# Linear attention and two dense layers on one core: a block's scores behind its outputs and state, five blocks ahead of the layers

## The chip, the cores and the metric

The kernel runs on one core of one Trainium2 chip. The metric is the device time in microseconds of one execution of the whole program. The engines of the core work side by side, each on a queue of its own: TensorE (PE) multiplies matrices, VectorE (DVE), ScalarE (ACT) and GpSimd (POOL) do the elementwise work, and SyncE (SP) starts the transfers. An instruction begins when those ahead of it on its engine have been issued and when the data and buffers that it needs are free; semaphores tell it so.

## The reference, cut to what matters

Attention runs in blocks of 64 positions with a state per head that decays from block to block; its output goes through two dense layers with different activations.

```python
for b in range(nb):                                  # 12 blocks of 64
    qb, kb, vb = (q[:, :, sl], k[:, :, sl], v[:, :, sl])
    intra = np.einsum('bhic,bhjc->bhij', qb, kb) * Dmask[None]
    intra = np.einsum('bhij,bhjd->bhid', intra, vb)
    inter = np.einsum('bhid,bhde->bhie', qb * lam_pow[None], kv_state)
    out[:, :, sl] = intra + inter
    kb_dec = kb * rev_pow[None]
    kv_state = lam_block[None, :, None, None] * kv_state + np.einsum('bhsd,bhse->bhde', kb_dec, vb)
...
x = out as (1536, 512)
h = x @ w_in;   x = np.where(h > 0, h, np.exp(np.minimum(h, 0)) - 1) @ w_out      # layer 1
h = x @ w2_in;  out = (np.maximum(h, 0) + alpha * np.minimum(h, 0)) @ w2_out      # layer 2
```

There are 2 sequences of 768 positions, 8 heads of 64; the layers are 512 to 2048 to 512 wide. The weights are doubles, the rest are floats.

## The kernel before

**Attention.** The recurrence does not depend on the block's length, and the kernel takes blocks of 128 positions: 12 of them, 6 for each sequence. Heads are taken in 4 pairs. For a block n, `scores` (L201, tile `sc`) multiplies keys and queries on PE into two PSUM banks, one for each head of the pairs; `mask` (L208, tile `sm`) multiplies each bank by the decay on DVE and frees it. `outputs` (tile `po`) adds on PE what comes from the state (L249, with the scaled queries `qs_t`) and what comes from the masked scores (L255). `keep` then splits the result in two parts of the type fp32r, which the layers multiply: ACT casts it to the high part `xh` (L267), DVE subtracts that to get the low part `xl` (L268). `state` (L222, tile `stp`) multiplies scaled keys `kd_t` and values on PE; ACT scales the old state (L230) and DVE adds the new part (L236), or copies it at a sequence's first block (L234). `scale` makes `kd_t` (L182) and `qs_t` (L189) on POOL. A block's keys and queries are one load of 0.5 MB, its values and natural keys a second one of 0.5 MB (0.25 MB in a sequence's last block).

**Layers.** Each layer has 4 groups of 4 chunks of the hidden width, 3 tiles of 512 tokens: 48 items a layer, 96 in all, in the order group, tile, chunk. An item's `up` is 12 matmuls of 512 columns (L355): high weights `wih` times high x, and the two mixed products `wil` times `xh` and `wih` times `xl`. ACT takes relu and exp (L366, L369), DVE makes `g_t` (L370), ACT its high part `gh_t` (L376), POOL its low part `gl_t` (L377). An item's `down`, two items later (LAG), is 12 matmuls of the same kind (L393, tile `dn`).

**Weights.** They come in 32 pieces of 1 MB, 8 for each of the four matrices, as pairs of 32-bit words of a double. `split_w` makes two float parts of such a piece with six operations: ACT scales the upper word (L125), DVE shifts and merges in three operations (L126, L128, L131, tile `wt`), ACT casts to the high part `wih` or `woh` (L134), POOL subtracts for the low part `wil` or `wol` (L135). The arguments `first` and `gaps` say how many ticks later each of the six is put in the program. Each piece's first matmuls in the layers wait for it; pieces 0 and 2 are the first two of `w_in`, 1 and 3 the first two of `w_out`.

**The order.** The program is written out in order, without a scheduler. A count of ticks goes up inside `up` (4 ticks), after each part of `down` (4 for an item), and a few times a block ahead of the layers; `later(n, step)` puts a step n ticks on. The first AHEAD blocks run before the first item; then each of the first items is `up(i)`, the block AHEAD + i, and `down(i - 2)`. `weights(i)` starts the splits of the table `when` at item i (negative ones during the blocks ahead), with the times of the table `early`, and the loads of later pieces.

**Buffers.** All eight PSUM banks are in one ring: scores take two, outputs, state and `up` one each, the `down` of four chunks of one tile four. A bank is given out again when the operations that read it are done: the masks for scores, cast and `xl` for outputs, addition or copy for state.

`begin` starts the loads, builds the decays (`dm` and `qp`, by scans on DVE), does scores, scaling and mask of block 0, the scaling of block 1, the state of block 0, and starts the split of piece 0. The functions that the change touches, and what calls them:

Of the kernel before, what the change touches and what calls it, by code (L numbers as in the profile page):

```python
# [15 lines left out]
NBLK = B * S // C  # L16
# [10 lines left out]
NG = 4  # L27
GF = NF // NG
LAG = 2
AHEAD = 4  # L30


@with_exitstack
def attention_two_layers(
# [13 lines left out]
    nc = tc.nc  # L48
# [16 lines left out]
    def bank(name):  # L65
        return ps.tile([128, 512], F32, tag="ps", name=name)
# [14 lines left out]
    def later(n, step):  # L81
        if n:
            due.setdefault(clock[0] + n, []).append(step)
        else:
            step()
# [52 lines left out]
    xh = {}  # L138
# [17 lines left out]
    st = [st2[:, 0], st2[:, 1]]  # L156
# [4 lines left out]
    def load(n):  # L161


        t = accp.tile([128, 4, 512], F32, tag="acc", name="blk")
        z = t[:, 0:2].rearrange("p s (a i) -> p s a i", a=NP)
        nc.sync.dma_start(out=z, in_=kqT[n])
        m = 2 if n % PB != PB - 1 else 1
        u = t[:, 2:4].rearrange("p s (h d) -> p s h d", h=H)
        nc.sync.dma_start(
            out=u[:, 0:m], in_=vk[n, :, 0:m, :].rearrange("j a (h d) -> j a h d", h=H))  # L170
        ld[n] = z
        vs[n] = (u[:, 0], u[:, 1] if m > 1 else None)
# [21 lines left out]
    def scores(n):  # L194
        z = ld[n]

        ps_ = [bank("sc"), bank("sc")]
        for pr in range(NP):
            for hs in range(2):
                a, b = hs * 64, (hs + 1) * 64  # L200
                nc.tensor.matmul(  # L201
                    out=ps_[hs][:, pr * C:(pr + 1) * C], lhsT=z[a:b, 0, pr, :],
                    rhs=z[a:b, 1, pr, :], start=True, stop=True)
        sc[n] = ps_

    def mask(n):
        for hs, p_ in enumerate(sc.pop(n)):
            nc.vector.tensor_tensor(  # L208
                out=sms[n % 2][:, hs], in0=p_.rearrange("p (a i) -> p a i", a=NP),
                in1=dm[:, hs], op=ALU.mult)  # L210
# [60 lines left out]
    def run_up(n):  # L271
        pw = bank("warm")
        for _ in range(n):
            nc.tensor.matmul(out=pw[:, 0:C], lhsT=warm, rhs=warm, start=True, stop=True)  # L274

    def block(n):

        if n + 1 < NBLK:
            scores(n + 1)
            mask(n + 1)  # L280
        keep(n, outputs(n))
        for _ in range(3 if n < AHEAD else 0):
            tick()
        if n + 1 < NBLK:
            state(n + 1)
        if n + 4 < NBLK:
            load(n + 4)
        if n + 2 < NBLK:
            scale(n + 2)

    def begin():
        nc.sync.dma_start(out=row[:, 128:128 + H], in_=lam.rearrange("h a -> a h"))
        load(0)
        load(1)
        load(2)
        load_w(0)
        load(3)
        nc.vector.memset(warm, 0.0)
        nc.vector.memset(row[:, 0:128], 1.0)

        nc.gpsimd.memset(anti, 0.0)
        nc.gpsimd.affine_select(
            out=anti, in_=anti, pattern=[[1, C]], base=1 - C, channel_multiplier=1,
            compare_op=ALU.not_equal, fill=1.0)
        nc.scalar.activation(fill[:, 0:1], warm[:, 0:1], AF.Exp)
        run_up(3)

        p_ = bank("lamp")
        nc.tensor.matmul(
            out=p_[:, 0:H], lhsT=row[:, 0:128], rhs=row[:, 128:128 + H], start=True, stop=True)  # L310
        run_up(5)
        nc.vector.tensor_copy(lam_sb, p_[:, 0:H])
        for hs in range(2):
            a, b = hs * 64, (hs + 1) * 64
            nc.vector.tensor_copy(
                lamp[a:b, 0:NP], lam_sb.rearrange("p (a s) -> p s a", s=2)[a:b, hs])


        for hs in range(2):
            for pr in range(NP):  # L320
                h = 2 * pr + hs
                nc.vector.tensor_tensor_scan(  # L322
                    out=dm[:, hs, pr, :], data0=lam_sb[:, h:h + 1].to_broadcast([128, C]),
                    data1=anti, initial=0.0, op0=ALU.mult, op1=ALU.add)

        for pr in range(NP):
            nc.vector.tensor_tensor_scan(
                out=qp[:, pr, :], data0=lamp[:, pr:pr + 1].to_broadcast([128, C]),
                data1=warm, initial=1.0, op0=ALU.mult, op1=ALU.add)
        for s_ in st:  # L330
            nc.gpsimd.memset(s_, 0.0)
        scores(0)
        scale(0)
        mask(0)
        scale(1)
        state(0)
        split_w(0, (8, 9, 11, 13, 15), 7)


    gh = {}  # L340
# [4 lines left out]
    def up(i):  # L345
        l, q, t, f = items[i]
        wh, wl = split[2 * (l * NPAIR + f // 2)]
        fo = (f % 2) * 128
        p_ = bank("up")
        n = 0  # L350

        rest = [(wl, xh), (wh, xl)]
        for w, x in [(wh, xh)] + (rest if f % GF == 0 else rest[::-1]):
            for cc in range(NCC):
                nc.tensor.matmul(  # L355
                    out=p_, lhsT=w[:, cc, fo:fo + 128], rhs=x[t][:, cc, :],
                    start=n == 0, stop=n == 3 * NCC - 1)
                n += 1
                if n % 3 == 0:
                    tick()  # L360
        g = tmp.tile([128, CH], F32, tag="g", name="g_t", bufs=3)
        r = tmp.tile([128, CH], F32, tag="r", name="r_t", bufs=3)
        gh_ = gp.tile([128, CH], F32R, tag="gh", name="gh_t")
        gl_ = gp.tile([128, CH], F32R, tag="gl", name="gl_t")
        gh[i], gl[i] = gh_, gl_
        nc.scalar.activation(r, p_, AF.Relu, scale=-1.0)  # L366
        if l == 0:

            nc.scalar.activation(r, r, AF.Exp, scale=-1.0)  # L369
            later(1, lambda: nc.vector.scalar_tensor_tensor(  # L370
                out=g, in0=r, scalar=-1.0, in1=p_, op0=ALU.add, op1=ALU.max))
        else:

            later(1, lambda: nc.vector.scalar_tensor_tensor(  # L374
                out=g, in0=r, scalar=beta[:, f:f + 1], in1=p_, op0=ALU.mult, op1=ALU.add))
        later(2, lambda: nc.scalar.copy(gh_, g))  # L376
        later(3, lambda: nc.gpsimd.tensor_tensor(  # L377
            out=gl_, in0=g, in1=gh_.bitcast(F32), op=ALU.subtract))
# [46 lines left out]
    PER = NCH * GF  # L425

    when = {-1: [2], 0: [1], 2: [3]}
    early = {2: ((6, 7, 9, 11, 13), 5), 1: ((2, 4, 6, 8, 10), 1)}
    for g in range(1, 2 * NG):
        o = (g - 1) * PER  # L430

# [4 lines left out]
    def weights(i):  # L436
        for c in when.get(i, []):
            split_w(c, *early.get(c, ()))
            if c + 3 < 4 * NPAIR:
                later(10, lambda c=c: load_w(c + 3))  # L440

    def parts(i, e):

# [3 lines left out]

    with tc.manual_schedule():
        begin()
        for n in range(AHEAD):  # L450
            weights(n - AHEAD)
            block(n)
# [6 lines left out]
        for i, _ in enumerate(items):  # L459
            if i == 2:  # L460
                nc.sync.dma_start(out=alpha_sb, in_=alpha)
            if i == 20:
                nc.vector.tensor_scalar(
                    out=beta, in0=alpha_sb, scalar1=-1.0, scalar2=1.0, op0=ALU.mult,
                    op1=ALU.add)
            n = AHEAD + i
            up(i)
# [63 lines left out]
```

## Time and profile before

| | before |
|---|---|
| median of 3 runs | 588.08 us (588.04 to 588.97) |
| profiled execution | 588.86 us, of which the span of the core's work 586.9 |
| PE | 573.2 us busy, 98% of the span, 2958 matmuls |
| weight loads of PE | 475.8 us, 81% (beside the matmuls) |
| DVE | 275.8 us, 47% |
| ACT | 240.9 us, 41% |
| POOL | 231.3 us, 39% |
| mean granted clock | 0.994 of full |

The busy shares are means over the span. Cut in 40 slices of 14.7 us, PE is at 80 to 90% in the first two, at 60% in the third and at 90% or more in nearly all others; the granted clock is full but for the first slice and the fifth (58.7 to 73.4 us). DVE and POOL are busiest, and the transfers fullest (331 to 415 GB/s), in the first three slices. What PE waits for thus lies in the first 60 us, where the 12 blocks, the loads and the first splits meet.

How to read the views used below: the list of waits has, for each engine and line, what ended its idle time, with the total in us, the number of times and the longest. The chain of work is followed back from the last instruction, and shows what ran one after the other up to there. A timeline lists the instructions of an engine with start and duration, and in brackets the idle time ahead and what ended it. A table of windows has busy times of stretches. "x16" for scores is 8 matmuls in 16 records.

### The profile page before, as it was taken

What the parts mean: (1) busy time and instruction counts of PE and PEld (TensorE: products, weight loads), DVE (VectorE), ACT (ScalarE), POOL (GpSimd) and SP (SyncE); (2) the same over time, 40 slices, a digit from 0 to 9 for tenths busy, and PEclk for the clock granted to TensorE, in tenths of its full rate; (3) what the DMA queues carried; (4) which work ended last, traced back from release to release, by engine and by line L of the source; (5) the groups of instructions that cost most, each with busy time, mean ns of one, the idle gap of its engine ahead of it and who ended that gap; (6) DMA issues with size and microseconds to landing.
All of it is one profiled execution on the core that took longest, in us unless ns stands there. A gap on an engine that the chain in (4) does not pass through costs nothing.

```text
span 586.9 us, 7331 instructions
## 1 busy us (share of the span) xinstructions
PE 573.2 (98%) x2958; PEld 475.8 (81%) x2958; DVE 275.8 (47%) x363; ACT 240.9 (41%) x374; POOL 231.3 (39%) x156
## 2 busy tenths in 40 slices
PE   8896999999999999999999999999999999999997
PEld 7685888888888888888888888888888888888886
DVE  7877343654535443453646632443543541541332
ACT  2645343656444444445554542443324322432220
POOL 4685421445333443443243444344325334432221
PEclk9999899999999999999999999999999999999999
DMA  8994200433102212221012222122203110000111
GB/s 331 415 353 162 69 1 1 143 95 120 43 29 73 71 73 71 73 71 73 16 56 71 73 71 73 71 74 71 73 0 126 30 60 0 2 0 1 71 73 71
DMA packets 18307, 49.23 MB, mean 84 GB/s; under 512 B 1250, under 2 KB 1506, under 8 KB 18274
## 3 DMA queue, kind: packets, MB, share of 16 engines
q1 hardware_dynamic: 18274, 48.77, 23.4%
q8 instruction: 23, 0.38, 0.2%
q14 instruction: 10, 0.08, 0.0%
HBM read 45.62 MB, written 3.15 MB: 83 GB/s over the span
## 4 chain that ended last, share of the span: by engine, by line
PE 92%; POOL 3%; DMA 2%; issue 1%; DVE 1%; ACT 0%; DVEq 0%; POOLq 0%; SPq 0%
PE dn L393 44%; PE up L355 43%; DMA blk<-in_kqT 2%; PE po L255 1%; POOL kd_t L182 1%; PE sc L201 1%; PE po L249 1%; POOL qs_t L189 1%; POOL gl_t L377 1%; PE stp L222 1%; DVE dm L322 0%; DVE acc L409 0%; POOL wol L135 0%; PE warm L274 0%; POOL wil L135 0%
## 5 line engine op out<-in xcount | busy, mean ns | idle before, releaser
L377 POOL TENSOR_TENSOR gl_t<-g_t,gh_t 128x512 fp32r<-128x512 f32 x96 | 125.7, 1309 | 327.3 <-ACT gh_t L376 274.6
L366 ACT ACTIVATE r_t<-up 128x512 f32<-128x512 f32 x96 | 57.3, 597 | 184.9 <-PE up L355 184.9
L376 ACT CAST gh_t<-g_t 128x512 fp32r<-128x512 f32 x96 | 59.6, 621 | 114.0 <-DVE g_t L370 60.9
L409 DVE TENSOR_TENSOR acc<-dn,acc 128x512 f32<-128x512 f32 (+1 forms) x73 | 47.0, 678 | 75.7 <-PE dn L393 75.7
L393 PE MATMUL dn<-gh_t,woh 128*128 128x512 f32 x192 | 76.3, 397 | 0.2 <-DVE xl L268 0.2
L374 DVE SCALAR_TENSOR_TENSOR g_t<-r_t,beta,up 128x512 f32<-128x512 f32 x48 | 35.7, 743 | 86.2 <-ACT r_t L366 77.4
L393 PE MATMUL dn<-gl_t,woh 128*128 128x512 f32 x192 | 75.5, 393 | 0.0
L393 PE MATMUL dn<-woh,gl_t 128*128 128x512 f32 (+1 forms) x196 | 75.5, 385 | 0.0
L393 PE MATMUL dn<-woh,gh_t 128*128 128x512 f32 (+1 forms) x196 | 75.5, 385 | 0.0
L393 PE MATMUL dn<-wol,gh_t 128*128 128x512 f32 (+1 forms) x196 | 75.4, 385 | 0.0
L393 PE MATMUL dn<-gh_t,wol 128*128 128x512 f32 x192 | 75.4, 393 | 0.0
L370 DVE SCALAR_TENSOR_TENSOR g_t<-r_t,up 128x512 f32<-128x512 f32 x48 | 32.9, 685 | 63.2 <-ACT r_t L369 58.7
L355 PE MATMUL up<-xh,wih 128*128 128x512 f32 x192 | 51.7, 391 | 0.0
L355 PE MATMUL up<-yh,wih 128*128 128x512 f32 x192 | 51.4, 389 | 0.0
L355 PE MATMUL up<-xl,wih 128*128 128x512 f32 x192 | 51.4, 389 | 0.0
L355 PE MATMUL up<-xh,wil 128*128 128x512 f32 x192 | 51.4, 389 | 0.0
L355 PE MATMUL up<-yl,wih 128*128 128x512 f32 x192 | 51.3, 389 | 0.0
L355 PE MATMUL up<-yh,wil 128*128 128x512 f32 x192 | 51.3, 389 | 0.0
L126 DVE TENSOR_SCALAR wt<-wt 128x1024 uint32<-128x1024 uint32 x32 | 31.4, 982 | 33.7 <-ACT wt L125 33.6
L393 PEld LDWEIGHTS dn<-gh_t,woh 128*128 128x128 f32 x192 | 36.6, 190 | 8.8 <-issue 0.6
L393 PEld LDWEIGHTS dn<-woh,gh_t 128*128 128x128 f32 x196 | 36.8, 188 | 7.4
L393 PEld LDWEIGHTS dn<-woh,gl_t 128*128 128x128 f32 x196 | 36.8, 188 | 7.4
(57 smaller groups left out, 797.2 us busy)
## 6 DMA issues: line engine op xcount, KB each, us to landing
raw<-in_w1i SPq DMA_DIRECT2D x8, 1024.0 KB, 5.8
raw<-in_w1o SPq DMA_DIRECT2D x8, 1024.0 KB, 4.8
raw<-in_w2i SPq DMA_DIRECT2D x8, 1024.0 KB, 5.3
raw<-in_w2o SPq DMA_DIRECT2D x8, 1024.0 KB, 4.8
blk<-in_kqT SPq DMA_DIRECT2D x12, 512.0 KB, 6.5
blk<-in_vk SPq DMA_DIRECT2D x10, 512.0 KB, 7.7
out<-acc SPq DMA_DIRECT2D x11, 256.0 KB, 2.1
blk<-in_vk SPq DMA_DIRECT2D x2, 256.0 KB, 6.4
```

Source lines behind the costliest of these rows:

```text
L126: later(gaps[0], lambda: nc.vector.tensor_scalar(out=tu, in0=tu, scalar1=3, scalar2=None, op0=ALU.logical_shift_left))
L182: nc.gpsimd.tensor_tensor(out=kd_.rearrange("p (a s) d -> p a s d", s=2), in0=kk.rearrange("p (a s) d -> p a s d", s=2), in1=rev.to_broadc ...
L189: nc.gpsimd.tensor_tensor(out=qs_, in0=q_, in1=qp, op=ALU.mult)
L201: nc.tensor.matmul(out=ps_[hs][:, pr * C:(pr + 1) * C], lhsT=z[a:b, 0, pr, :], rhs=z[a:b, 1, pr, :], start=True, stop=True)
L355: nc.tensor.matmul(out=p_, lhsT=w[:, cc, fo:fo + 128], rhs=x[t][:, cc, :], start=n == 0, stop=n == 3 * NCC - 1)
L366: nc.scalar.activation(r, p_, AF.Relu, scale=-1.0)
L370: later(1, lambda: nc.vector.scalar_tensor_tensor(out=g, in0=r, scalar=-1.0, in1=p_, op0=ALU.add, op1=ALU.max))
L374: later(1, lambda: nc.vector.scalar_tensor_tensor(out=g, in0=r, scalar=beta[:, f:f + 1], in1=p_, op0=ALU.mult, op1=ALU.add))
L376: later(2, lambda: nc.scalar.copy(gh_, g))
L377: later(3, lambda: nc.gpsimd.tensor_tensor(out=gl_, in0=g, in1=gh_.bitcast(F32), op=ALU.subtract))
L393: nc.tensor.matmul(out=p_, lhsT=a, rhs=b, start=first and n == 0, stop=last and n == 2)
L409: nc.vector.tensor_tensor(out=a, in0=p_, in1=a, op=ALU.add)
```

## The change

Four things are moved; no arithmetic is added or taken away.

- **Scores.** `block(n)` did scores and mask of block n+1 ahead of the outputs of block n. Now it does so only for n < AHEAD; from there on they stand behind the state of block n+1, that is last in the block on PE, and the mask stands behind `xl` and the state addition on DVE. Scores and mask of block 1 go into `begin`, ahead of the first state; the scans for `qp` go behind the mask of block 0.
- **AHEAD** is 5 instead of 4, so item i goes with block i + 5.
- **First weights.** The split of piece 0 starts 16 ticks on instead of 7, behind the fourth block; block 3 is loaded ahead of piece 0. The splits of pieces 2 and 1 have new times in `early`, and since piece 2's start is tied to AHEAD it comes one block later too. Later weight loads are issued 11 ticks behind a split's start instead of 10.
- **Order within `up`.** The two mixed products came with `wil` first in each group's first chunk and with `xl` first otherwise; now `wil` comes first only in the first chunk of the second layer.

```diff
-AHEAD = 4
+AHEAD = 5
...
+    def next_scores(n):
+        if 1 < n < NBLK:
+            scores(n)
+            mask(n)
+
     def block(n):
 
-        if n + 1 < NBLK:
-            scores(n + 1)
-            mask(n + 1)
+
+        if n < AHEAD:
+            next_scores(n + 1)
         keep(n, outputs(n))
         for _ in range(3 if n < AHEAD else 0):
             tick()
         if n + 1 < NBLK:
             state(n + 1)
+        if n >= AHEAD:
+            next_scores(n + 1)
         if n + 4 < NBLK:
             load(n + 4)
...
         load(2)
+        load(3)
         load_w(0)
-        load(3)
...
-        for pr in range(NP):
-            nc.vector.tensor_tensor_scan(
-                out=qp[:, pr, :], data0=lamp[:, pr:pr + 1].to_broadcast([128, C]),
-                data1=warm, initial=1.0, op0=ALU.mult, op1=ALU.add)
         for s_ in st:
             nc.gpsimd.memset(s_, 0.0)
         scores(0)
         scale(0)
         mask(0)
+
+        for pr in range(NP):
+            nc.vector.tensor_tensor_scan(
+                out=qp[:, pr, :], data0=lamp[:, pr:pr + 1].to_broadcast([128, C]),
+                data1=warm, initial=1.0, op0=ALU.mult, op1=ALU.add)
         scale(1)
+        scores(1)
+        mask(1)
         state(0)
-        split_w(0, (8, 9, 11, 13, 15), 7)
+        split_w(0, (17, 18, 19, 20, 22), 16)
...
-        for w, x in [(wh, xh)] + (rest if f % GF == 0 else rest[::-1]):
+        for w, x in [(wh, xh)] + (rest if l and q == 0 and f == 0 else rest[::-1]):
...
-    early = {2: ((6, 7, 9, 11, 13), 5), 1: ((2, 4, 6, 8, 10), 1)}
+    early = {2: ((7, 8, 10, 12, 14), 6), 1: ((2, 3, 4, 6, 8), 1)}
...
-                later(10, lambda c=c: load_w(c + 3))
+                later(11, lambda c=c: load_w(c + 3))
```

What this does to the engines' queues shows at three places. Line numbers of the layers are 9 higher behind the change.

The first is PE at the second item. In the order before, its `up` is followed by the scores of block 6, then the outputs of block 5 and the state of block 6:

```order
L355 MATMUL up<-xh_204,wih 128x512 x4
L355 MATMUL up<-xl_205,wih 128x512 x4
L355 MATMUL up<-xh_204,wil 128x512 x4
L201 MATMUL sc<-blk 128x128 x8
L249 MATMUL po<-qs_t,st 128x128 x4
L255 MATMUL po<-sm,blk 64x128 x8
L222 MATMUL stp<-blk,kd_t 64x64 x8
```

In the changed order, the first item's `up` comes with block 5, and its scores for block 6 are last:

```order
L364 MATMUL up<-xh_204,wih 128x512 x4
L364 MATMUL up<-xl_205,wih 128x512 x4
L364 MATMUL up<-xh_204,wil 128x512 x4
L249 MATMUL po<-qs_t,st 128x128 x4
L255 MATMUL po<-sm,blk 64x128 x8
L222 MATMUL stp<-blk,kd_t 64x64 x8
L201 MATMUL sc<-blk 128x128 x8
```

The scores moved from ahead of the outputs to behind the state, and the same block goes with an item that is one earlier.

The second is DVE around the split of the first output weights. Before, the three operations on `wt_415` come behind an item's `g_t`, and the mask of block 6 (into `sm_95`), the `xl` of block 5 and the state's copy follow:

```order
L370 SCALAR_TENSOR_TENSOR g_t_409<-r_t_410,up_392 128x512
L126 TENSOR_SCALAR wt_415<-wt_415 128x1024
L128 SCALAR_TENSOR_TENSOR wt_415<-raw_284,wt_415 128x1024
L131 SCALAR_TENSOR_TENSOR wt_415<-raw_284,wt_415 128x1024
L208 TENSOR_TENSOR sm_95<-sc_481,dm_94 128x512
L208 TENSOR_TENSOR sm_95<-sc_482,dm_94 128x512
L268 TENSOR_TENSOR xl1_444<-po_493,xh1_443 128x4x128
L234 COPY st_97<-stp_508 64x4x64 x2
```

Now the copy and the mask of block 6 come ahead of the same split (on `wt_447`), and `xl` of block 6, the state addition and the mask of block 7 (into `sm_96`) follow it:

```order
L268 TENSOR_TENSOR xl1_416<-po_450,xh1_415 128x4x128
L234 COPY st_97<-stp_465 64x4x64 x2
L208 TENSOR_TENSOR sm_95<-sc_476,dm_94 128x512
L208 TENSOR_TENSOR sm_95<-sc_477,dm_94 128x512
L379 SCALAR_TENSOR_TENSOR g_t_441<-r_t_442,up_425 128x512
L126 TENSOR_SCALAR wt_447<-wt_447 128x1024
L128 SCALAR_TENSOR_TENSOR wt_447<-raw_281,wt_447 128x1024
L131 SCALAR_TENSOR_TENSOR wt_447<-raw_281,wt_447 128x1024
L268 TENSOR_TENSOR xl1_416<-po_527,xh1_415 128x4x128
L236 TENSOR_TENSOR st_97<-stp_538,st_97 64x4x64 x2
L208 TENSOR_TENSOR sm_96<-sc_553,dm_94 128x512
L208 TENSOR_TENSOR sm_96<-sc_554,dm_94 128x512
```

Each mask moved from ahead of an `xl` and a state addition to behind them, and with that one block deeper in the queue.

The third is POOL at the low half of the second input weights. Before, `wil_340` comes behind the scaling of block 6's keys and ahead of the first item's `gl_t`:

```order
L182 TENSOR_TENSOR kd_t_450<-blk_331,dm_94 128x512
L135 TENSOR_TENSOR wil_340<-wt_338,wih_339 128x1024
L377 TENSOR_TENSOR gl_t_412<-g_t_409,gh_t_411 128x512
L182 TENSOR_TENSOR kd_t_522<-blk_383,dm_94 128x512
L189 TENSOR_TENSOR qs_t_524<-blk_383,qp_93 128x512
```

Now it (`wil_389`) comes behind the scaling of block 7 and behind that `gl_t`:

```order
L182 TENSOR_TENSOR kd_t_422<-blk_325,dm_94 128x512
L182 TENSOR_TENSOR kd_t_491<-blk_379,dm_94 128x512
L189 TENSOR_TENSOR qs_t_493<-blk_379,qp_93 128x512
L386 TENSOR_TENSOR gl_t_444<-g_t_441,gh_t_443 128x512
L135 TENSOR_TENSOR wil_389<-wt_387,wih_388 128x1024
L135 TENSOR_TENSOR wol_449<-wt_447,woh_448 128x1024
```

The low half and the first item's `gl_t` have changed places, and the two low halves now stand one behind the other.

## Rows read from the trace of the kernel before

**Rows 1.** Waits of PE: engine line, waited for, total us, times, longest.

```profile
PE stp L222 <- issue: 4.8, 1, 4.8
PE stp L222 <- POOL kd_t L182: 2.5, 2, 1.3
PE sc L201 <- DMA blk<-in_kqT: 1.4, 1, 1.4
```

**Rows 2.** Chain of work, PE's pieces: start us, us, what.

```profile
11.33 1.09 PE sc L201 x16
...
57.95 1.12 PE stp L222 x16
59.07 4.71 PE dn L393 x12
63.78 2.72 PE up L355 x12
66.50 1.09 PE sc L201 x16
...
68.68 1.02 PE po L255 x16
...
70.17 2.94 PE dn L393 x12
```

**Rows 3.** Windows: busy us of PE, PEld, DVE, ACT, POOL; clock; DMA; GB/s.

```profile
20.00:30.00 10.00, 8.62 (x94) 7.00 (x91) 9.11 (x14) 6.48 (x14) 7.99 (x6) 1.00 1.03 418
60.00:62.00 2.00, 2.00 (x6) 1.59 (x5) 0.74 (x2) 1.20 (x2) 0.50 (x1) 0.50 0.94 365
```

**Rows 4.** Timeline of DVE and POOL ahead of the long stop: start us, us, instruction.

```profile
52.21 0.83 DVE L126 TENSOR_SCALAR wt<-wt 128x1024 uint32<-128x1024 uint32 x1 [1.73 <-ACT wt L125]
...
52.45 1.50 POOL L182 TENSOR_TENSOR kd_t<-blk,dm 128x512 f32<-128x512 f32 x1
...
53.08 1.96 DVE L128 SCALAR_TENSOR_TENSOR wt<-raw,wt 128x1024 uint32<-128x1024 uint32 x1
...
53.92 2.24 POOL L189 TENSOR_TENSOR qs_t<-blk,qp 128x512 f32<-128x512 f32 x1
...
55.07 2.17 DVE L131 SCALAR_TENSOR_TENSOR wt<-raw,wt 128x1024 uint32<-128x1024 uint32 x1
57.17 1.28 DVE L208 TENSOR_TENSOR sm<-sc,dm 128x512 f32<-128x512 f32 x2
```

**Rows 5.** Timeline: durations of single operations of ACT, DVE and POOL.

```profile
15.06 1.13 ACT L125 ACTIVATE wt<-raw 128x1024 f32<-128x1024 f32 x1
...
16.22 0.69 DVE L126 TENSOR_SCALAR wt<-wt 128x1024 uint32<-128x1024 uint32 x1 [0.33 <-ACT wt L125]
...
27.84 1.23 DVE L128 SCALAR_TENSOR_TENSOR wt<-raw,wt 128x1024 uint32<-128x1024 uint32 x1
...
40.52 1.05 ACT L134 CAST woh<-wt 128x1024 fp32r<-128x1024 f32 x1 [5.71 <-DVE wt L131]
...
41.66 2.37 POOL L135 TENSOR_TENSOR wol<-wt,woh 128x1024 fp32r<-128x1024 f32 x1
...
42.63 0.57 ACT L267 CAST xh<-po 128x512 fp32r<-128x512 f32 x1
...
43.23 0.69 DVE L268 TENSOR_TENSOR xl<-po,xh 128x512 fp32r<-128x512 f32 x1 [1.55 <-ACT xh L267]
...
46.14 1.29 POOL L377 TENSOR_TENSOR gl_t<-g_t,gh_t 128x512 fp32r<-128x512 f32 x1 [2.11 <-ACT gh_t L376]
...
47.59 1.28 ACT L230 ACTIVATE st<-st,qp 128x128 f32<-128x128 f32 x4
...
48.91 0.86 DVE L236 TENSOR_TENSOR st<-stp,st 64x256 f32<-64x256 f32 x2 [0.48 <-ACT st L230]
```

**Rows 6.** Timeline of POOL: key scalings that a load released.

```profile
9.40 1.06 POOL L182 TENSOR_TENSOR kd_t<-blk,dm 128x512 f32<-128x512 f32 x1 [1.77 <-DMA blk<-in_vk]
...
29.25 1.99 POOL L182 TENSOR_TENSOR kd_t<-blk,dm 128x512 f32<-128x512 f32 x1 [2.00 <-DMA blk<-in_vk]
```

## The prediction

> **What bounds the kernel now.** I read the busy times by stage first: TensorE (PE) is busy for nearly the whole span, so the time is PE's work plus what PE loses while it waits or runs at a lower clock. The list of PE's waits [rows 1] says where: 4.8 us once, 2.5 us on the key scaling `kd_t`, 1.4 us on a load. The chain of work [rows 2] puts the 4.8 us ahead of the state matmuls that start at 57.95; after them nothing holds PE any more. All that matters therefore lies ahead of the fifth `up`, which starts at 63.78 [rows 2]; I call it up(4), and number items and blocks from 0. From there on before and after run the same matmuls, with PE as the bound.
>
> Full-speed pieces of PE come from the same rows: scores 1.09, the part of a block's outputs from the state 1.09 (68.68 less 66.50 less 1.09), the part from its scores 1.02, state 0.47 (what is left until 70.17), together 3.67 a block; `up` 2.72, `dn` 2.94. The long stop costs twice: after it the granted clock is 0.50, which is 1.2 of 2.4 GHz [rows 3]; the state matmuls take 1.12 instead of 0.47 and `dn` 4.71 instead of 2.94 [rows 2], 2.4 us more.
>
> What causes the stop is in the rows of VectorE (DVE) and GpSimd (POOL) [rows 4]: PE waits for a PSUM bank that the mask of block 8 frees, and that mask stands on DVE behind the three operations of a weight split. These take turns with POOL's. The split's first operation ends at 53.04; `kd_t`, issued at 52.45, ends 0.91 after that; the second, issued at 53.08, ends 1.09 after `kd_t`; `qs_t` 1.12 after the second; the third 1.08 after `qs_t`. Alone they take 0.69 and 1.23 [rows 5]; in turns the three last 5.03. Whichever is issued second waits for nearly all of the other. The Trainium skill, SBUF — State Buffer, section Who interferes with whom, says the same as a rule: two such operations share a port pair as an exclusive lock that the first one keeps for its whole instruction. The trace agrees, and the rule speaks against a change that queues more splits in a row on the path to a mask; what the sum would be without it stands with the rivals.
>
> **The change part by part.** It removes three waits, moves one, and makes a new chain.
>
> *Start.* Keys and queries of block 3 are loaded ahead of the first weights, 1 MB earlier: the 1.4 us wait goes. The first split leaves POOL's way to `kd_t` of block 4, and the larger part of the 2.5 us goes. Scores of block 1 move ahead of the state matmuls of block 0, but its second load lands at 9.40 [rows 6] and the first one a transfer earlier, so PE is again done with the state of block 1 at 11.33 [rows 2]. The `qp` scans stand behind a mask now; the first `qs_t` still waits for POOL's `kd_t` (9.40 and 1.06), so this costs nothing while that covers it, and about 1.3 us, one mask, if not. Blocks 1 to 3 then need 3 x 3.67: PE ends the state of block 4 at 22.3.
>
> *Block 5's scores* now come ahead of `up`. Their load: block 6's second half lands at 29.25 [rows 6], with 2.36 MB behind block 5's first half, 5.6 us at 418 GB/s [rows 3], so it lands at 23.6. PE waits 1.3; block 4's outputs end at 26.8.
>
> *The first weights.* From the end of block 2's outputs on PE (18.2) ACT does a cast 0.57, the state scaling 1.28 and the split's scaling 1.13, until 21.2. DVE's three split operations find one `qs_t` running (until 22.2) and have a mask 1.28 and an `xl` 0.69 between them: 27.2. ACT's cast 1.05 gives the high half at 28.2, POOL 2.37 later the low half, 30.6 [rows 5]. PE waits 1.4 and 0.6; up(0) ends at 31.5.
>
> *The chain behind it.* Now the mask of block n+1 stands behind `xl` of block n and the state addition, and both stand behind splits. ACT scales the state until 29.5. DVE: addition 0.86, mask 1.28, `xl` 0.69 to 32.4; the split of the second w_in pair with the rest of a `kd_t` and one `qs_t` between, 4.6, to 37.0; `xl`, the copy that stands for the addition, mask, and `g_t`, as long as an `xl`, to 40.5. PE, from 31.5 with 2.11 + 0.47 + 1.09 + 2.72, wants block 6's mask at 37.9; its halves are there at 39.2 and 39.85: 1.8 lost.
>
> *The split of the first w_out pair* follows at 40.5. Its first operation ends at 41.2; `gl_t` of item 0 runs on POOL until 42.4 (cast 0.6 and 1.29); the second operation until 43.5; then POOL's low half of the second w_in pair, queued behind that `gl_t` though it could run earlier, until 45.7; then the third, until 46.8. PE reaches the last third of up(2), which needs that low half, at 44.1: 1.6 lost. ACT's w_out cast waits for the third operation, as its 5.71 us of idle time show in the trace of before, and the next item's two activations and the cast of block 6's outputs stand behind it: 2.7 [rows 5], 49.5; state scaling 1.28, addition 0.86, first half of block 7's mask 0.64: 52.3. PE stands at block 7's outputs from 47.7 on: 4.6, and 0.5 for the second half. Queued behind it on PE are everything of items 2 and 3. Such a stop brought the half clock in before; I take the same 2.4 us.
>
> *The moved stop.* The masks, `g_t`, casts and scalings of one more item and block take DVE and ACT from 52.9 to 61.7; then the split of the second w_out pair, 5.03 as in [rows 4], and `xl` of block 8, until 67.5. It frees the bank for the second half of block 9's scores. PE, from 53.8 with 0.47 + 1.09 + 2.94 + 2.72 + 2.11 + 0.47 + 0.14 and the 2.4 of the clock, is there at 66.2: 1.3 lost. So the loss by the clock costs nothing more: without it the wait would be 3.7.
>
> *Sum.* Rest of the scores 0.95, `dn` 2.94: up(4) starts at 71.4, with one block more done than in before. Before, with that block: 63.78 + 3.67 = 67.45. That is 3.95 later. Block 10's scores wait in the same way for `xl` of block 9, which needs up(4), two activations, a cast and itself: 0.7. Together **4.65 us**. The profiled execution took 588.86 us for a span of 586.9, so it would take 593.5; the median of the runs is 588.08, so I predict **592.8 us**, +0.8%.
>
> *At no cost:* the order of the two low products in `up` (same twelve matmuls, and no wait of PE from 64 us on [rows 1]); the later second and third w_out loads and the blocks' loads queued behind them on SP (SP waits for the first split until 27.2, and block 8's data, issued then, is wanted by POOL after 46 us; were that cover gone, some 8 us of transfer).
>
> **The rivals.** (a) *DVE and POOL take other turns.* If the third w_out operation gets in front of the low half, it ends at 44.6 instead of 46.8; block 7 then waits 1.7 instead of 5.1, PE's clock holds there, and the moved stop becomes 3.8. If the clock holds there too, up(4) starts 2.2 earlier: 590.5. For it: issue times lie 0.1 us apart. Against: if the clock falls at the second stop, the gain is gone and it is my forecast. (b) *Both stops halve the clock*: 2.4 more, 595.2. For it: the second is my least certain term; against: after a first loss it is short. (c) *Faster*: the operations that I let take turns do not meet. Then the splits take 3.15 each, block 7's mask is ready some 5 us earlier and the moved stop ends another 1.9 earlier; PE's own work sets most of the pace, up(4) starts near 65.4, and with 2.0 less than before the time is 586. It decides if block 7's mask comes before about 47 us. For it: scores behind the state take away the reason of the old stop, and in before POOL is idle for stretches; against: in [rows 4] every meeting costs its turn, and DVE's order leaves no way around the splits. Without the exclusive turns the sum would be this, with them it is mine. (d) *No change*: a milder (a) with a shorter low half; 588.
>
> **How the numbers follow.** Forecast 0.58 (591.3 to 594.8), (a) 0.14, (b) 0.10, (c) 0.12, (d) 0.06. A measurement of this kernel tells about 0.2% from no change, 1.2 us. Faster 0.12, within 0.06, slower 0.82. Leaving out (c), (d) and the far end of (b) gives 590.0 to 596.5: below it are the port's other turns with a held clock, above it two clock losses with a full 5 us wait.
>
> **What the profile will show.** Right, if PE's waits hold one of 4 to 5 us ahead of the second part of block 7's outputs near 48 us, released by DVE's mask, with a granted clock of 0.5 behind it, waits of 1 to 2 us on the low half of the second w_in pair and on block 6's mask, and one on `xl` in block 9's scores; and no wait on block 3's load nor on `kd_t` of block 4. Wrong, if the split's operations on DVE between 40 and 47 us last 0.7 and 1.2 us, if block 7's mask stands ahead of PE, or if up(4) starts before 67 us.

## The result and the profile after

The changed kernel took 592.5 us (median of 8 runs, 590.2 to 594.3), the kernel before, run beside it, 588.9 (588.0 to 591.5): a ratio of 1.0052, with a 95% interval of 1.0028 to 1.0077. It is slower, by 3.6 us between the medians and 3.1 by the ratio (1.6 to 4.5 by its interval). The forecast was 592.8 with a range of 590.0 to 596.5. The traced execution took 590.50 us for a span of 588.5, against 588.86 and 586.9 before, so what follows from this one trace explains 1.6 us, and the rest has to come from how executions differ. The slice in which PE was at 60% in the kernel before is the fourth of the 40 (44.0 to 58.7 us), not the third; the long stop lies in it.

PE's waits of the changed kernel come first: engine, line, what was waited for, total us, times, longest.

```profile
PE sc L201 <- DVE xl L268: 3.6, 2, 3.1
PE sc L201 <- DMA blk<-in_kqT: 2.9, 3, 1.4
PE up L364 <- POOL wil L135: 2.6, 2, 2.2
PE po L255 <- DVE sm L208: 2.3, 4, 1.2
...
PE up L364 <- ACT wih L134: 1.0, 1, 1.0
```

The 4.8 us ahead of the state and the 2.5 us on key scalings of [rows 1] are gone. What came in their place is spread over five kinds of waits, none as long as the old one. The same waits in PE's timeline (start, us, instruction, in brackets the idle time and what ended it) show where most of them lie:

```profile
23.65 1.16 PE L201 MATMUL sc<-blk 64*128 64x128 f32 x16 [1.25 <-DMA blk<-in_kqT]
...
27.94 1.20 PE L364 MATMUL up<-xh,wih 128*128 128x512 f32 x4 [1.01 <-ACT wih L134]
...
30.42 1.20 PE L364 MATMUL up<-xh,wil 128*128 128x512 f32 x4 [0.37 <-POOL wil L135]
...
38.84 0.43 PE L255 MATMUL po<-sm,blk 128*64 128x128 f32 x2 [0.77 <-DVE sm L208]
...
46.33 1.19 PE L364 MATMUL up<-xh,wil 128*128 128x512 f32 x4 [2.23 <-POOL wil L135]
...
49.62 0.43 PE L255 MATMUL po<-sm,blk 128*64 128x128 f32 x2 [1.21 <-DVE sm L208]
...
64.45 1.16 PE L201 MATMUL sc<-blk 64*128 64x128 f32 x14 [3.09 <-DVE xl L268]
...
74.61 1.16 PE L201 MATMUL sc<-blk 64*128 64x128 f32 x14 [0.53 <-DVE xl L268]
```

From top to bottom: block 5's load, high and low half of the first weights, block 6's mask, the low half of the second w_in pair in up(2), block 7's mask, the second bank of block 9's scores, and that of block 10's. Each of these places was in the prediction. Not shown are two more waits on loads, 1.39 us for block 1's, where the kernel before waited 1.28 for `kd_t`, and 0.22 for block 4's. One of the forecast waits was far smaller than forecast: 1.21 (and 0.17 on the second half) ahead of block 7's outputs, where 4.6 and 0.5 with a half clock behind were expected. One was larger: 3.09 in block 9's scores, where 1.3 was expected.

The chain of work behind that last stop (start, us, what) ends at up(4), at 68.56:

```profile
63.71 0.69 DVE xl L268
64.40 0.04 issue
64.45 1.16 PE sc L201 x14
65.60 2.96 PE dn L402 x12
68.56 2.72 PE up L364 x12
```

In the prediction's terms the kernel before would be there, with one block more done, at 67.45. So 1.1 us were lost up to here, and 0.5 more in block 10's scores: the 1.6 us between the two spans. The down behind the stop takes 2.96, full speed: in this execution the clock did not fall at all.

### The profile page after: what moved, and what is told of

Read it like the earlier page. It is cut to its first block, busy times and chain, and to the rows that moved or that the text cites. A ratio compares the mean times of both kernels' runs of the same rounds, so it can differ in the third digit from the quotient of the medians.

```text
span 588.5 us, 7329 instructions
## 1 busy us (share of the span) xinstructions
PE 571.4 (97%) x2958; PEld 474.9 (81%) x2958; DVE 274.5 (47%) x363; ACT 241.3 (41%) x374; POOL 230.0 (39%) x156
## 4 chain that ended last, share of the span: by engine, by line
PE 91%; DVE 4%; ACT 2%; DMA 1%; issue 1%; POOL 0%; SPq 0%; DVEq 0%
PE dn L402 44%; PE up L364 43%; PE sc L201 1%; PE po L255 1%; DMA blk<-in_kqT 1%; PE po L249 1%; DVE wt L128 1%; DVE sm L208 1%; ACT st L230 1%; DVE wt L131 1%; POOL wil L135 0%; DVE acc L418 0%; ACT wt L125 0%; DVE wt L126 0%; PE stp L222 0%
## 5 line engine op out<-in xcount | busy, mean ns | idle before, releaser
L126 DVE TENSOR_SCALAR wt<-wt 128x1024 uint32<-128x1024 uint32 x32 | 29.5, 923 | 32.8 <-ACT wt L125 32.8
L364 PEld LDWEIGHTS up<-xh,wil 128*128 128x128 f32 x192 | 35.9, 188 | 10.8 <-POOL wil L135 3.4
L364 PEld LDWEIGHTS up<-xh,wih 128*128 128x128 f32 x192 | 35.8, 188 | 8.8 <-ACT wih L134 1.3
```

What stands on the lines that cost most here:

```text
L126: later(gaps[0], lambda: nc.vector.tensor_scalar(out=tu, in0=tu, scalar1=3, scalar2=None, op0=ALU.logical_shift_left))
L364: nc.tensor.matmul(out=p_, lhsT=w[:, cc, fo:fo + 128], rhs=x[t][:, cc, :], start=n == 0, stop=n == 3 * NCC - 1)
```

## Experiments

**Two more executions of the changed kernel.** Nothing is edited; each run gives the trace of another execution.

> The changed kernel once more, for the trace of another execution; its eight times lie between 590.2 and 594.3 us, the traced one took 590.5. Theory of the turns: executions differ in which operation comes first where VectorE and GpSimd meet at 40 to 47 us. In an execution of 592 us or more GpSimd's low half of the second w_in pair comes ahead of the third operation of the first w_out split; that operation then ends near 46.5 instead of 44.1, and TensorE waits 4 to 5 us ahead of block 7's outputs instead of 1.4, with a granted clock of 0.5 behind it. Rival, the clock alone: the turns are as traced (third operation done at 44.1, a wait of 1.4), and a slow execution differs only by a half clock behind the 3.1 us stop in block 9's scores.

> As the run before it: the changed kernel in a further execution. Turns: a time near 590.5 goes with the third operation done at 44.1 us, one of 592 or more with about 46.5. Clock alone: 44.1 in both, and the time follows the granted clock behind the stop in block 9's scores.

They took 593.03 and 592.07 us. Both have the turns of the first trace: the third operation of the split lasts 2.19 and the waits behind it are 2.21, 1.21 and 0.17. So the theory of the turns, by which a slow execution is one in which DVE and POOL meet in the other order, fell. In the chain of the second of them the stop in block 9's scores ends at the same time as above, and then:

```profile
64.43 1.16 PE sc L201 x14
65.59 4.54 PE dn L402 x12
70.12 2.76 PE up L364 x12
```

The down takes 4.54 instead of 2.96. The table of windows (busy us and count of PE, PEld, DVE, ACT, POOL; clock; DMA share; GB/s) shows the stretch of the first trace, at full clock, and that of this one, where it is close to 0.5 (1.2 of 2.4 GHz):

```profile
66.00:70.00 4.00, 4.00 (x20) 3.26 (x19) 1.31 (x3) 1.57 (x2) 1.95 (x2) 1.00 0.59 223
```

```profile
66.00:70.00 4.00, 4.00 (x13) 3.11 (x12) 1.30 (x3) 1.57 (x2) 1.97 (x2) 0.57 0.61 226
```

4.54 less 2.96 is 1.58; 592.07 less 590.50 is 1.57. Here the clock alone is the whole difference. The other execution lost the same 1.58 behind block 9's scores, and 0.9 more by the time it was there. Its loss began at the start: block 1's load came later, its scores started at 8.55 instead of 7.88, and the clock fell there as well, which it did not in the first trace (8 to 12 us, first this execution, then the first trace):

```profile
8.00:12.00 4.00, 3.45 (x40) 3.23 (x42) 2.79 (x7) 0.00 (x0) 2.19 (x2) 0.60 1.03 419
```

```profile
8.00:12.00 4.00, 4.00 (x80) 3.69 (x80) 3.81 (x9) 1.34 (x4) 2.40 (x3) 1.00 1.01 411
```

In the three traces the spread is thus mostly one question: does the clock fall behind a stop of 3.1 us or not. The same stop did both. This does not explain all of the eight times: 1.58 is less than half of the 4.1 us between the fastest and the slowest, and the mean clock alone does not put them in order (591.0 us at 0.993, 592.5 at 0.997). What the executions without a trace lost beyond it is not shown.

**ScalarE's cast later.**

```diff
-    early = {2: ((7, 8, 10, 12, 14), 6), 1: ((2, 3, 4, 6, 8), 1)}
+    early = {2: ((7, 8, 10, 12, 14), 6), 1: ((2, 3, 4, 9, 11), 1)}
```

> The changed kernel with ScalarE's cast of the first w_out pair and GpSimd's low half 3 ticks later, so that they stand behind the next item's activations, the cast of block 6's outputs and the state scaling instead of ahead of them. Theory (block 7's mask is late because ScalarE's cast, held by the split, stands ahead of block 6's cast): the mask ends near 47 instead of 50.2 us and the 1.2 and 0.2 us ahead of block 7's outputs go. With the turns of the traced execution 590.5 becomes 589.1; the stop in block 9's scores grows to about 4 us, since TensorE is there sooner, and may cost the clock: 588.5 to 591.5 over all. Rival, the first weights and loads at the start (block 5's load 1.25 us, high and low half 1.0 and 0.4) make the loss: no change from the changed kernel, 590.2 to 594, median 592.5.

Measured: 590.8 us (589.3 to 591.9), ratio 1.0020 (1.0008 to 1.0032). The mask of block 7 ended at 47.96 instead of 50.16 and the waits ahead of block 7's outputs are gone, as expected; the stop in block 9's scores, expected to grow to about 4 us, was 1.99 in the trace:

```profile
62.69 1.16 PE L201 MATMUL sc<-blk 64*128 64x128 f32 x14 [1.99 <-DVE xl L268]
```

DVE's chain came earlier too, which the expectation left out: `xl` of block 8 ended at 62.65 instead of 64.40, while PE was there at 60.70 instead of 61.36. Behind this stop the granted clock was 0.50 from 64 to 66 us, and the 12 down matmuls took 4.54. The rival, by which nothing changes, does not fit the waits that went nor the median, 1.7 us lower; the two intervals of the ratio just touch. Part of the gain is given back at the next stop.

**The scores ahead again.** One part of the change undone:

```diff
-        if n < AHEAD:
-            next_scores(n + 1)
+        next_scores(n + 1)
...
-        if n >= AHEAD:
-            next_scores(n + 1)
```

> The changed kernel with one part undone: scores and mask of the next block ahead of the outputs for all blocks, as in the kernel before; five blocks ahead, load order and split times stay. Theory (the loss comes from the splits that stand in VectorE's queue ahead of whatever TensorE waits for, not from the place of the scores): the waits on the masks of blocks 6 and 7 (0.9 and 1.4 us) and on xl in blocks 9 and 10 (3.1 and 0.5) go, and a stop of 4 to 5 us comes back at the state of block 9, behind the second w_out split, with a half clock worth 2.4: 590.5 to 592, no gain on the median of the changed kernel beyond 1.5 us. Rival (scores behind outputs and state make the loss): 588 or less, as before.

Measured: 587.5 us (586.2 to 589.0), ratio 0.9973 (0.9960 to 0.9986), faster than before. Here my theory missed and the rival was right on the total: by the ratios, without the moved scores the change gains 1.6 us, with them it loses 3.1. The waits say why the expected stop did not come back:

```profile
PE up L361 <- POOL wil L135: 3.9, 2, 3.5
PE sc L201 <- DMA blk<-in_kqT: 1.5, 2, 0.8
PE up L361 <- ACT wih L134: 1.3, 1, 1.3
...
PE stp L222 <- issue: 0.6, 1, 0.6
```

The stop at the state is there, but only 0.6 long. PE waits 3.5 for the low half in up(2) and then runs behind it at half clock, which the window shows:

```profile
48.00:50.00 2.00, 2.00 (x17) 1.78 (x18) 1.61 (x4) 0.35 (x3) 2.00 (x3) 0.50 0.62 221
```

It comes so late to the state of block 9, at 62.03, that the split ahead of the mask is done (at 61.93), and only the mask itself is left to wait for. The stop that scores behind the state could remove is thus mostly covered by the delay of PE ahead of it, and what the move adds (2.3 on masks, 3.6 on `xl`) is more than what it takes off (0.6 at the state, 1.3 of the wait on the low half and the half clock behind it).

**The scores behind alone.** The same move made in the kernel before, with nothing else of the change:

```diff
-        if n + 1 < NBLK:
+        if n + 1 < NBLK and n < AHEAD:
             scores(n + 1)
             mask(n + 1)
         keep(n, outputs(n))
...
             state(n + 1)
+        if n + 1 < NBLK and n >= AHEAD:
+            scores(n + 1)
+            mask(n + 1)
```

> The kernel before with one part of the change alone: from item 0 on the scores and mask of the next block stand behind its outputs and state; four blocks ahead, load order and split times as before. Theory (scores behind the state lose by themselves, because their mask then comes behind xl, the state addition and a split on VectorE, and TensorE is back for it after one up): the 4.8 us stop at the state of block 8 goes, and in its place come a wait of 4 to 5 us ahead of block 6's outputs, one of 2 to 4 in block 8's scores and two of 0.5 to 0.8 in those behind: 590 to 593. Rival (they lose only together with the fifth block ahead and the new split times): no slower than before, 586 to 588.5.

Measured: 589.8 us (589.5 to 591.8), ratio 1.0024 (1.0014 to 1.0033): slower than before, just under the theory's lower end. Its long waits:

```profile
PE po L255 <- DVE sm L208: 3.5, 2, 3.3
PE sc L201 <- DVE xl L268: 2.7, 3, 1.6
```

Both kinds are where the theory put them, at 3.3 where it said 4 to 5, at 1.6 where it said 2 to 4. Against the 4.8 us and 2.4 us of half clock that it removes, the move pays 6.2 us of waits, and half clock again behind the 3.3 (0.50 from 46 to 48 us). So the two parts don't add: -0.27% for the rest of the change and +0.24% for the scores, but +0.52% together. The traces show why: with either part alone the 4.8 us stop is gone or down to 0.6, so both remove the same stop.

**The second w_out split later.**

```diff
-    early = {2: ((7, 8, 10, 12, 14), 6), 1: ((2, 3, 4, 6, 8), 1)}
+    early = {2: ((7, 8, 10, 12, 14), 6), 1: ((2, 3, 4, 6, 8), 1),
+             3: ((9, 10, 11, 12, 13), 3)}
```

> The changed kernel with the split of the second w_out pair later: its three VectorE operations behind block 8's xl and state addition and block 9's mask. Theory (the 3.1 us stop in block 9's scores waits for xl of block 8 behind that split, and the clock falls or not behind this stop, which makes the spread from 590.2 to 594.3): the stop shrinks to about 1 us, one of about 2 comes in block 10's scores, the granted clock stays at 1.0 behind both: 589.5 to 590 in nearly every execution, a spread under 1.5 us. Rival (the clock falls for what lies earlier, such as the waits of 2.2 and 1.2 us at 44 to 50 us): half clock in some executions and a spread of 3 us as before, median 591.5 or more.

Measured: 589.0 us (588.4 to 591.5), ratio 1.0008 (0.9996 to 1.0020). The two waits on `xl` became 0.53 and 1.02, where about 1 and 2 were expected, and ten of twelve executions lie between 588.4 and 589.7. Two took 591.2 and 591.5 at a mean clock of 0.993: the clock can fall elsewhere too, which is the rival's part.

**GpSimd's scaling out of the way.**

```diff
-        if n + 2 < NBLK:
+        if n + 2 < NBLK and n != 8:
             scale(n + 2)
+        if n == 7:
+            scale(10)
...
-            qs_ = small.tile([128, NP, C], F32, tag="qs", name="qs_t")
+            qs_ = small.tile([128, NP, C], F32, tag="qs", name="qs_t", bufs=3)
```

> The changed kernel with GpSimd's scaling of keys and queries of block 10 one item earlier (and a third buffer for scaled queries), so that GpSimd does nothing while VectorE splits the second w_out pair near 60 us. Theory (the two engines take exclusive turns): the second and third operation of that split last 1.25 us each instead of 1.96 and 2.17, xl of block 8 comes 1.6 us earlier, the stop in block 9's scores shrinks from 3.1 to about 1.5, the clock holds: about 589 us. Rival (the operations are as long there for another reason): 2.0 and 2.2 as before, stop 3.1, 590 to 594.

Measured: 589.2 us (588.9 to 590.8), ratio 1.0012 (1.0003 to 1.0022). DVE's timeline of the split, with POOL idle from 60 to 64 us:

```profile
59.96 1.23 DVE L128 SCALAR_TENSOR_TENSOR wt<-raw,wt 128x1024 uint32<-128x1024 uint32 x1
61.22 1.22 DVE L131 SCALAR_TENSOR_TENSOR wt<-raw,wt 128x1024 uint32<-128x1024 uint32 x1
```

In the changed kernel the same two took 1.96 and 2.17, beside `kd_t` and `qs_t`. Nothing but POOL's work was moved from there, so the turns are shown, not only read. In this traced execution the clock fell earlier, near 48 us, behind the wait of 2.2 us that ended at 46.66. Windows of it:

```profile
48.00:50.00 2.00, 1.22 (x8) 0.92 (x6) 1.64 (x4) 0.28 (x1) 2.00 (x3) 0.53 0.62 225
50.00:52.00 2.00, 2.00 (x17) 1.69 (x19) 1.08 (x2) 0.88 (x2) 1.37 (x2) 0.50 0.00 0
```

That made PE later at block 9's scores, and the stop there 0.53, where 1.5 was expected. It also held the cast of block 8's outputs, so `xl` of block 8 came only 0.23 us earlier than in the changed kernel (at 63.48), though the split was done at 62.44 instead of 63.79.

**All but the scores, with splits moved.** From the kernel with the scores ahead, steps of three splits are moved (called sa_best below):

```diff
-    early = {2: ((7, 8, 10, 12, 14), 6), 1: ((2, 3, 4, 6, 8), 1)}
+    early = {2: ((7, 8, 10, 12, 12), 6), 1: ((2, 3, 4, 9, 11), 1),
+             3: ((9, 10, 11, 12, 13), 3)}
```

> All but one part of the change (scores ahead of the outputs for all blocks, as in the kernel before), with three splits' steps moved: low half of the second w_in pair 2 ticks earlier, so ahead of the first gl_t on GpSimd; ScalarE's cast and GpSimd's low half of the first w_out pair 3 ticks later; the second w_out split behind the next g_t. Theory (what is left of the loss is splits queued ahead of what TensorE waits for): the 3.5 us wait on the low half goes with its half clock of about 1.7, the stop at the state of block 9 goes, waits of 0.7 to 1 us stay on block 7's outputs and on two down products: 587.5 less 4.5, about 583 us. Rival (the scores' place alone matters, the waits move on): 586 to 588.

> sa_best once more, on the same chip as the three ahead of it, for comparison with them: 583 to 584 as measured; about 1.3 us above before_s3w if the fifth block ahead costs what its waits at the start say (block 5's load, first weights: 0.7, 1.3 and 0.4 us, against a key scaling and a load before).

Measured: 583.4 us (582.9 to 583.9), ratio 0.9908 (0.9895 to 0.9922), and in the second comparison 583.2, 0.9893 (0.9873 to 0.9912). Of the waits expected to stay, 0.9 on block 7's outputs and 0.7 on one down product are left, and the mean granted clock is 0.997 or more in every execution. It stands 1.1 us above the last kernel below, where 1.3 was expected.

**The whole change with splits moved.** The same line of `early`, with the scores behind outputs and state as in the change.

> The whole change (scores behind outputs and state, five blocks ahead) with the three moves of splits that sa_best has. Theory (scores behind lose by themselves even with the splits out of the way: each item's up is all the cover that a mask has, and the second bank of block 9's and 10's scores waits for an xl): waits of 0.8 ahead of block 7's outputs, 0.5 and 1.0 in the scores of blocks 9 and 10, 0.9 on block 6's mask, clock held: 586 to 586.5, some 3 us above sa_best. Rival (with the splits out of the way the place of the scores is free): 583 to 584.

Measured: 586.7 us (586.3 to 587.0), ratio 0.9953 (0.9937 to 0.9969). Its waits behind the start:

```profile
PE po L255 <- DVE sm L208: 2.2, 4, 1.3
...
PE sc L201 <- DVE xl L268: 1.6, 2, 1.1
```

With the splits out of the way, scores behind still cost 3.4 us (586.7 less 583.2), as the theory said. Its reason, that an `up` is all the cover that a mask has, holds for the first two masks: PE waits 0.54 and 1.31 for those of blocks 6 and 7, and for none later, where a `down` stands between as well. The other waits left behind the start are those on `xl`, 1.6 us.

**The kernel before with splits moved.** Nothing of the change; first one split (before_s3), then two (before_s3w):

```diff
-    early = {2: ((6, 7, 9, 11, 13), 5), 1: ((2, 4, 6, 8, 10), 1)}
+    early = {2: ((6, 7, 9, 11, 13), 5), 1: ((2, 4, 6, 8, 10), 1),      # before_s3
+             3: ((9, 10, 10, 12, 13), 3)}
...
+    early = {2: ((6, 7, 9, 11, 13), 5), 1: ((2, 4, 6, 9, 11), 1),      # before_s3w
+             3: ((9, 10, 10, 12, 13), 3)}
```

> The kernel before, with nothing of the change, and the split of the second w_out pair later: its VectorE operations behind the mask of block 8, its cast and low half as late as they can be for the down that needs them. Theory (the 4.8 us stop at the state of block 8 and the half clock behind it, 7.2 us together, come from that split's place in VectorE's queue alone): both go; a wait of about 1.7 us comes on the low half in the down of item 2: near 583.5. Rival (the scores ahead of outputs hold the bank, so the stop comes back elsewhere): 587 or more.

> As before_s3, and ScalarE's cast of the first w_out pair behind the next item's activations and block's cast. Theory: the small waits at 43 to 50 us go too, 582 to 582.5 us, faster than every kernel with a part of the change. Rival: the cast is covered there, same as before_s3.

Measured: 582.9 us, ratio 0.9888 (0.9869 to 0.9908), with one split moved; 582.1 us (582.0 to 582.2), ratio 0.9875 (0.9853 to 0.9898), with two, the fastest kernel of all. The list of PE's waits in the last one's trace:

```profile
PE stp L222 <- POOL kd_t L182: 2.3, 2, 1.2
PE sc L201 <- DMA blk<-in_kqT: 1.4, 1, 1.4
PE warm L274 <- DVE warm L298: 1.1, 1, 1.1
PE dn L393 <- POOL wol L135: 0.7, 1, 0.7
PE po L249 <- POOL qs_t L189: 0.2, 1, 0.2
```

The 4.8 of [rows 1] is gone, the key scalings and block 3's load are as they were, and 0.7 came on a low half. With one split moved the stop is gone as well, and the low half costs 0.68, where 1.7 was expected: 4.8 and 2.4 less 0.7 make the 6.5 us between the medians (589.3 and 582.9). The stop and its half clock belonged to the place of one split in DVE's queue. The change moved everything around it instead. The second moved split gave another 0.8 us by the medians; of the 0.9 between the two traces' spans, 0.5 lies at 43 to 53 us, where the theory put it, and 0.4 ahead of it, where the two kernels are alike.

## Why the prediction was right, and where it was not

The time, the sign and, roughly, the size held. The way to them held in part. Of the prediction's own signs, the main one did not come: no wait of 4 to 5 us ahead of block 7's outputs, and no half clock behind it. The waits on the low half (2.23, where 1 to 2 was said) and on `xl` came, the one on block 6's mask was smaller than its 1 to 2 us, and up(4) started at 68.56, not before 67. Of the split's operations between 40 and 47 us two lasted 0.68 and 1.22, as if alone, and the third 2.19.

*The start* came out as worked out. PE was done with the state of block 1 at 11.10 (11.33 forecast), waited 1.25 for block 5's load (1.3) until 23.65 (23.6), 1.01 and 0.37 for the first weights (1.4 and 0.6), and was done with up(0) at 31.6 (31.5). No wait on block 3's load or on `kd_t` of block 4 was left; the 0.22 on block 4's load was not foreseen.

*The chain behind it*: 0.77 and 0.16 on block 6's mask, where 1.8 was forecast. The low half held PE until 46.33; forecast were 44.1 and 1.6 more.

*The split of the first w_out pair* is the step that failed, with the sentence "`gl_t` of item 0 runs on POOL until 42.4 ...; the second operation until 43.5". It put `gl_t` ahead of the second operation. DVE and POOL in the trace of the changed kernel:

```profile
39.90 0.68 DVE L126 TENSOR_SCALAR wt<-wt 128x1024 uint32<-128x1024 uint32 x1
40.61 1.22 DVE L128 SCALAR_TENSOR_TENSOR wt<-raw,wt 128x1024 uint32<-128x1024 uint32 x1
...
40.72 2.26 POOL L386 TENSOR_TENSOR gl_t<-g_t,gh_t 128x512 fp32r<-128x512 f32 x1 [5.11 <-ACT gh_t L385]
...
41.87 2.19 DVE L131 SCALAR_TENSOR_TENSOR wt<-raw,wt 128x1024 uint32<-128x1024 uint32 x1
...
42.94 3.33 POOL L135 TENSOR_TENSOR wil<-wt,wih 128x1024 fp32r<-128x1024 f32 x1
```

The second operation was issued 0.11 us ahead of `gl_t` and went first. `gl_t` then took 2.26, the third operation its turn behind it, until 44.06, and the low half the one after that. The rule of turns is as forecast; their order is another one, with the third operation ahead of the low half as in rival (a), which gave 44.6 for the third operation, 1.7 for block 7, 3.8 for the moved stop and 590.5 for the time. The trace has 44.06, 1.4, 3.09 and 590.50 (and 0.53 in block 10's scores, forecast 0.7). All three traces have this order, so it is not a matter of one execution.

*The moved stop* was mis-sized with it. Since PE was not held at block 7, it reached block 9's scores at 61.4 instead of 66.2; `xl` of block 8 ended at 64.4 instead of 67.5; so it waited 3.09 instead of 1.3.

*The clock* brought the time back to the forecast. I let it fall behind block 7, for 2.4 us. In two of the three traces it falls behind block 9's scores instead, for 1.58, which I had written as what speaks against rival (a). Of the eight times two, 590.2 and 590.5, go with a mean clock of 1.000; the six others, 591.0 to 594.3, with 0.990 to 0.997, and the median lies among these. That the median is 0.3 from the forecast is partly luck, in two ways. A loss that did not come was made up for by others at other places: the second of the two further executions, which lost nothing at the start, is 1.4 below the sum (592.07 against 593.5). And the forecast stands on a time before of 588.08 (with its 4.65 us that makes 592.7, a rounding below 592.8), while the kernel before took 588.9 beside the changed one: as a difference, 4.65 was forecast and 3.6 measured.

*The other rivals.* (b), both stops at half clock, was not seen in a trace of the changed kernel. (c) was out: the operations met at every place named. The Trainium skill, SBUF — State Buffer, section Who interferes with whom, has it that the port pair which the two engines share is an exclusive lock, kept for the whole instruction, and that issue order decides who blocks; the trace agrees, with 0.11 us of lead turned into 0.97 us for the one behind (`gl_t` from 1.29 [rows 5] to 2.26), and the run with POOL out of the way takes the effect off (1.22 instead of 2.17).

*What the prediction did not see*: the parts of the change work against each other. And it followed where the old stop goes, but not that its cause, three operations whose result no matmul needs before the down of item 2, could have been moved itself: the run with only that split moved took 582.9.

**What stays open.** Load order, scans, `AHEAD` and first split time were only tried together: with the splits moved, the kernel with five blocks ahead takes 583.2 and the one with four 582.1, and which of these parts makes the 1.1 us was not tried; the two also differ in which splits are moved. The order of the two low products in `up` was not tried alone either. And why the clock falls behind one 3.1 us stop and not behind another of the same length, is not settled, nor what the untraced executions of the changed kernel lost.

## What to carry to other kernels

When the bound engine waits for a small operation, look at what is queued ahead of it, and ask when that is needed: moving one split behind the mask that PE waited for gained 6.5 us (ratio 0.9888), while reordering the small operations around it lost 3. Two edits that remove the same stop don't add, so cost each with the other in place. Where two engines share turns, work out both orders when the issue times lie within a few tenths of a microsecond, and name both times.

## What was not expected of the hardware

The granted clock behind a stop is not the same in each execution. Behind the same 3.1 us stop, at the same place of the program, it stayed at 1.00 in one traced execution and fell to about 0.5 in two, which cost 1.58 us each time. It also fell behind shorter ones: 2.21 us in the run with the scaling out of the way, where the same wait of 2.2 us left it at 1.00 in the three traces of the changed kernel; 1.99 us in that with ScalarE's cast later; 1.88 us on block 1's load in the first further execution. It did not fall at once: in the second execution of the changed kernel PE went on at 64.43, and the clock was at 1.00 until 66 us. The kernels whose longest wait behind the first 30 us is at most 1.3 us were the steady ones: mean clocks of 0.997 or more, and times within 1.0 us of each other (582.0 to 582.2, 582.7 to 583.1, 582.7 to 583.9, 586.3 to 587.0), while the changed kernel's lie over 4.1 us.

A late load can cost nothing: in the second run of the kernel with scores ahead and splits moved, block 5's load held PE 2.28 us instead of 0.68, the wait for the first weights then was 0.24 instead of 1.30, and up(0) began at 28.41 instead of 28.40.
